# Chunked attention feeding a routed expert layer on one core: the last tiles reordered

## The chip, the cores and the metric

The kernel runs on one core of a Trainium2 chip. The metric is the device time of one execution in microseconds (us); below it is the median of several runs. The core has five engines, each with its own queue of instructions that it works off in order: PE (TensorE, matrix products; its weight loads are listed as PEld), DVE (VectorE), ACT (ScalarE), POOL (GpSimd) and SP (SyncE, which here only issues transfers). Transfers run on 16 DMA engines, and are issued by SP or by POOL.

## The reference

Four sequences of 768 positions with 8 heads of 64 go through attention in chunks of 32 queries. A chunk sees 8 memory rows and the keys from 16 before the chunk to 8 behind it. The result, 3072 tokens of 512 numbers, goes through a dense layer of two products and, beside it, through one of eight experts per token.

```python
k_full = np.concatenate([mem_k, k_ctx], axis=2)        # per chunk of 32 queries
a = softmax(scale * q_c @ k_full.T); out_c = a @ v_full
...
x = out.transpose(0, 2, 1, 3).reshape(B * S, H * D)    # 3072 x 512
y_dense = np.maximum(x @ w1_dense, 0.0) @ w2_dense
logits = x @ w_gate                                    # 8 experts
expert_idx = np.argmax(logits, axis=1); probs = softmax(logits)
y_moe[mask] = gate_w[mask, None] * (np.maximum(x[mask] @ w1[e], 0) @ w2[e])
return y_dense + y_moe
```

## The kernel before, in words

**Tiles.** The 3072 tokens are 24 tiles of 128. A loop over g = 0 to 23 (L507 to L560) does one step for each of several tiles at once: `scores` and `exp` of tile g, `turn` (transposing the softmax weights) of g-1, `values` (attention times v, normalized into `xn`, cast by POOL into a ring row) of g-2, `turn_x` and `cast_x` (transposing the token rows for the products) of g-3, and `gate` (router logits), `dense1` and `dense2` of g-4. The order in which these are written is the order in each engine's queue; nothing reorders it. What is left of the last four tiles after g = 23 is written out by hand behind the loop (L567 to L657); this is called the tail below.

**Groups.** Tiles are routed in groups, before the change seven of three, then one of two and one of a single tile (L43). When the last tile of a group has its logits, `choose` (L366) finds each token's expert as a one-hot `oh` and the weight (`es`, and its reciprocal into the ring row), all on DVE but for one exponential on ACT. `rank` (L395) counts, with products on PE, how many earlier tokens chose the same expert (`oh_sum` holds the sums over earlier groups), adds the expert's first row (`ecap`), masks by `oh` and so has each token's row in `xs`, a table in DRAM with 3200 rows per expert. `ship` (L429) lets POOL scatter one tile's rows to `xs` by an indirect transfer. Tiles below 20 (`SPLIT`) go whole, with their dense result; of tiles 20 to 23 the token part goes first and the dense part by a late scatter (L657) once `dense2` is done.

**Buffers.** The ring has six rows, so the cast of tile t waits for the scatter of tile t-6. `xn` has one buffer: the next tile's `xn` waits for the cast and for the transposes of the one before. The values' PSUM tile `xp` has one buffer too.

**Loads.** POOL issues keys and queries, and from g = 6 one half of an expert's weights per iteration (`load_w`, L545: float32 in DRAM, bfloat16 in SBUF, 16 halves). SP issues v. In iterations 18 and 20 SP also issues the front writes (L552): 128 rows ahead of each expert's tokens in `xs` are filled with finite numbers, so that a slot which begins below an expert's first token reads something harmless.

**Table and slots.** Behind the last rank, products with `ones` give the tokens per expert (L617), and about a dozen small DVE operations (L621 to L644) and a product (L646) make a table of 31 slots: first row in `xs` and expert number. Each slot is 128 rows of one expert. SP reads row numbers from the table into its registers in batches (L673: two, then six, then eight), and fetches the rows (L695). For slots 0 to 3 the token part is fetched first (L792) and the dense part after the late scatters (L794); slot 4 and later are fetched whole. A slot is turned on PE (L718), goes through its expert's two products (L741, L754), is weighted and added to the dense part by DVE (L762) and scattered to the output by POOL (L764). 27 slots are always done; four more stand behind a test that is not met here.

Of the kernel before, what the change touches and what calls it, by code (L numbers as in the profile page):

```python
# [24 lines left out]
NT = B * TPB  # L25
# [17 lines left out]
GROUPS = [3] * (NT // 3 - 1) + [2, 1]  # L43
QKB = 6
SPLIT = 20
FAR = 1.0e6
# [3 lines left out]
def kernel(  # L50
# [44 lines left out]
    ecap = const.tile([128, E], F32, name="ecap")  # L95
    oh_sum = const.tile([128, GRP, E], BF16, name="oh_sum")
# [7 lines left out]
    def constants():  # L104
# [4 lines left out]
        for e in range(E):  # L109
            nc.vector.memset(prio[:, e:e + 1], float(E - e))  # L110
            nc.vector.memset(ecap[:, e:e + 1], float(e * SPAN + 128))
        nc.gpsimd.iota(tok, [[128, NT]], base=0, channel_multiplier=1)
# [5 lines left out]
    with ExitStack() as one:  # L118
# [125 lines left out]
        def attention(g, qT, kbd):  # L244
# [98 lines left out]
            def last(part):  # L343
                if u == grp["size"] - 1:
# [4 lines left out]
                    "dense2": dense2, "choose": lambda: last(choose),  # L349
# [16 lines left out]
        def choose(grp):  # L366
# [6 lines left out]
            def st(shape, name, dt=F32):  # L373
                return small.tile(shape, dt, tag=f"{name}{k}", name=name, bufs=2 if k == GRP else 1)
# [15 lines left out]
            es = st([128, k], "es")  # L390
            nc.vector.reduce_sum(es, ex, axis=AX.X)
            nc.vector.reciprocal(grp["row"][:, :k, GW], es)
            grp["oh"] = oh

        def rank(grp):  # L395
# [5 lines left out]
            def st(shape, name, dt=F32):  # L401
                return small.tile(shape, dt, tag=f"{name}{k}", name=name, bufs=2 if k == GRP else 1)


            nc.tensor.matmul(rk, upper, oh, start=True, stop=False)
# [8 lines left out]
            nc.vector.tensor_tensor(at, rk, ecap.unsqueeze(1).to_broadcast(SH), ALU.add)  # L414
            nc.vector.tensor_tensor(at, at, oh, ALU.mult)
# [4 lines left out]
            nc.vector.tensor_tensor(oh_sum[:, :k], oh_sum[:, :k], oh, ALU.add)  # L420
# [40 lines left out]
        low = const.tile([128, E, E], F32, name="low")  # L461
        rb = const.tile([128, NSLOT + 1], F32, name="rb")

        def table_constants():
# [4 lines left out]
            nc.vector.memset(low, 0.0)  # L469
            for e in range(1, E):  # L470
                nc.vector.memset(low[:, e, :e], 1.0)
# [35 lines left out]
        for g in range(NT):  # L507
# [16 lines left out]
            do("choose", 4)  # L524
            do("dense1", 4)
# [19 lines left out]
            if g >= 6:  # L545
                load_w()
# [5 lines left out]
            if g in (18, 20):  # L552

                for e in range(g % 4 // 2, E, 2):
# [278 lines left out]
```

## Time and profile before

| | |
|---|---|
| time, median of 3 runs | 266.5 us (265.94 to 268.05) |
| the profiled execution | 267.22 us, of which 265.3 are its span |
| PE, PEld busy | 211.3, 169.1 us |
| DVE, ACT, POOL busy | 171.5, 148.2, 145.1 us |
| mean granted clock of PE | 0.929 |
| weight loads (POOL) | 16 of 512 KB, 9.5 us from issue to landing |
| scatters to `xs` | 28, median 3.6 us |
| fetches of whole slots | 23 of 385 KB, median 4.4 us |

The profile is taken on the chip in one execution. It has a page and a trace that answers questions. In the page and the answers, L12 is line 12 of the kernel before, and times are us from the start of the span. A row of the timeline has start, length, engine, line, operation, output and inputs with shape, count, and in brackets how long the engine had been idle and what ended it. A row of the chain of waits has start, length, engine and work; the chain follows the work that ended last back to what released it. Lines marked "issue" are time for which the profile names no cause. A row of stretches has the busy time of each engine in that stretch, the clock granted to PE as a share of its full speed, the mean busy share of the DMA engines and the GB/s they moved.

### The profile page before, as it was taken

How to read it: one execution, taken by the hardware profiler on the slowest of the kernel's cores; microseconds unless marked ns; L12 is line 12 of the kernel's file. 1: busy time of each engine (PE TensorE's matmuls, PEld its weight loads, DVE VectorE, ACT ScalarE, POOL GpSimd, SP SyncE). 2: the span in 40 equal slices, each digit the busy share in tenths (PEclk: the TensorE clock that was granted, in tenths of full speed). 3: DMA queues.
4: the chain of work that ended last, by engine and by line, in shares of the span. 5: the costliest groups of instructions: out<-in, count | busy, mean ns of one | idle time of the engine just before them, and what ended most of it. 6: DMA issues, size and time to landing. Idle time of an engine off the chain costs nothing.

```text
span 265.3 us, 9665 instructions
## 1 busy us (share of the span) xinstructions
PE 211.3 (80%) x3936; PEld 169.1 (64%) x3969; DVE 171.5 (65%) x415; ACT 148.2 (56%) x232; POOL 145.1 (55%) x178
## 2 busy tenths in 40 slices
PE   0554898998988799877998699689558799999960
PEld 0343686777776688665886577678446577776730
DVE  6737677778785678774686946544633576776750
ACT  3744567778777667755767467313235455655520
POOL 8997394627868335635436434316541466565660
PEclk9999999999999889997999979755988999999995
DMA  5999999868999998997999999204267899999740
GB/s 78 194 198 196 193 201 194 149 112 169 152 224 231 237 199 200 181 216 147 150 215 353 303 227 175 91 2 161 80 190 223 281 292 327 310 327 314 243 158 28
DMA packets 55948, 52.52 MB, mean 198 GB/s; under 512 B 30302, under 2 KB 48222, under 8 KB 55904
## 3 DMA queue, kind: packets, MB, share of 16 engines
q0 software_dynamic: 22768, 31.52, 56.0%
q1 hardware_dynamic: 33136, 20.38, 32.4%
q8 instruction: 32, 0.52, 0.8%
q14 instruction: 12, 0.10, 0.1%
HBM read 48.74 MB, written 19.69 MB: 258 GB/s over the span
## 4 chain that ended last, share of the span: by engine, by line
PE 42%; DMA 26%; ACT 9%; DVE 9%; issue 7%; POOL 3%; SPq 2%; POOLq 0%; DVEq 0%; ACTq 0%
DMA vw<-in_v_dram 8%; DMA xg<-xs 6%; PE pgt L323 6%; PE ph L741 6%; PE py L754 5%; DMA wall<-in_moe_w_dense_dram 5%; PE py L339 5%; PE ph L330 5%; PE xp L292 4%; DMA xs<-wall 3%; PE ap L280 3%; PE xtp L311 3%; ACT vw L200 3%; PE tp L226 3%; ACT h L333 2%
## 5 line engine op out<-in xcount | busy, mean ns | idle before, releaser
L764 POOL DMA_INDIRECT out_dram<-o,dest x27 | 31.8, 1179 | 29.1 <-DVE o L762 27.2
L304 POOL CAST ring<-xn 128x512 bf16<-128x512 f32 x24 | 16.1, 669 | 55.5 <-DVE xn L301 52.2
L447 POOL DMA_INDIRECT xs<-ring,si x28 | 29.8, 1063 | 21.6 <-DVE oh_sum L420 7.5
L318 DVE CAST xT<-xtp 128x512 bf16<-128x512 f32 x24 | 16.6, 690 | 27.8 <-ACT x L313 27.8
L762 DVE SCALAR_TENSOR_TENSOR o<-py,xg 128x512 f32<-128x512 f32 x27 | 20.3, 751 | 18.0 <-PE py L754 14.9
L292 PE MATMUL xp<-vw,aT 64*32 64x65 f32 x1536 | 24.0, 239 | 9.1 <-issue 6.9
L741 PE MATMUL ph<-xT,wa 128*128 128x128 bf16 x432 | 29.3, 222 | 1.1 <-ACT xT L720 1.1
L323 PEld LDWEIGHTS pgt<-wgate,x 128*128 128x128 f32 x192 | 27.5, 217 | 3.4 <-issue 1.8
L323 PE MATMUL pgt<-wgate,x 128*128 128x8 f32 x192 | 28.0, 273 | 1.2 <-DVE df L380 1.2
L330 PE MATMUL ph<-xT,wall 128*128 128x128 bf16 x384 | 27.2, 227 | 1.6 <-issue 1.6
L741 PEld LDWEIGHTS <-wa 128*128 128x128 bf16 x432 | 26.2, 100 | 1.6 <-issue 1.4
L330 PEld LDWEIGHTS <-wall 128*128 128x128 bf16 x384 | 25.3, 106 | 2.7 <-issue 2.4
L754 PE MATMUL py<-wall,h 128*128 (+1 forms) x97 | 26.1, 379 | 1.0 <-issue 0.5
L292 PEld LDWEIGHTS xp<-vw,aT 64*32 64x32 f32 x1536 | 18.6, 112 | 12.9 <-issue 8.4
L339 PE MATMUL py<-wall,h 128*128 128x512 bf16 x74 | 22.3, 410 | 4.3 <-ACT h L333 1.4
L720 ACT COPY xT<-xt 128x512 bf16<-128x512 bf16 x27 | 15.7, 587 | 16.2 <-PE xt L718 16.2
L237 ACT COPY kbd<-tp 64x768 bf16<-64x768 bf16 x16 | 12.7, 792 | 20.0 <-PE tp L226 18.6
L744 ACT ACTIVATE h<-ph 128x512 bf16<-128x512 f32 x27 | 16.1, 597 | 11.3 <-PE ph L741 10.9
L731 DVE COPY wa<-wall 128x2048 bf16 (+1 forms) x27 | 18.4, 685 | 5.2 <-PE ph L741 3.9
L282 ACT COPY aT<-ap 128x512 f32<-128x512 f32 x24 | 14.0, 583 | 13.4 <-PE ap L280 13.3
L275 ACT ACTIVATE a<-a 128x512 f32<-128x512 f32 x24 | 15.1, 631 | 10.0 <-DVE a L270 9.9
L200 ACT COPY vw<-vw 24x1408 f32<-24x1408 f32 x15 | 20.5, 1365 | 0.4
(119 smaller groups left out, 428.3 us busy)
## 6 DMA issues: line engine op xcount, KB each, us to landing
xg<-xs SPq DMA_DIRECT2D x23, 385.0 KB, 4.4
wall<-in_moe_w_dram POOLq DMA_DIRECT2D x16, 512.0 KB, 9.5
xs<-wall SPq DMA_DIRECT2D x8, 385.0 KB, 11.7
kb<-in_k_dram POOLq DMA_DIRECT2D x16, 192.0 KB, 7.7
qb<-in_q_dram POOLq DMA_DIRECT2D x16, 192.0 KB, 8.2
vw<-in_v_dram SPq DMA_DIRECT2D x32, 96.0 KB, 7.4
vw<-in_v_dram SPq DMA_DIRECT2D x32, 88.0 KB, 10.1
wall<-in_moe_w_dense_dram POOLq DMA_DIRECT2D x2, 512.0 KB, 12.5
```

Of the source, the lines that this page charges most:

```text
L200: copy(vw[r + 32:r + CTX, hps, :VC - 1, :D], vw[r:r + CTX - 32, hps, 1:, :D])
L292: nc.tensor.matmul(xp[32 * cc:32 * cc + 32, par, (D + 1) * hp:(D + 1) * (hp + 1)], st["aT"][r, hp, 32 * cc:32 * cc + 32], vw[r, hp, 4 * (g ...
L318: nc.vector.tensor_copy(xT, st["xtp"])
L323: nc.tensor.matmul(grp["pg"][:, u, :], st["x32"][:, d, :], wgate[:, d, :], start=(d == 0), stop=(d == DT - 1))
L330: nc.tensor.matmul(ph[:, f, :], wall[:, E, d, 128 * f:128 * f + 128], st["xT"][:, d, :], start=(d == 0), stop=(d == DT - 1))
L339: nc.tensor.matmul(py, st["h"][:, f, :], wall[:, E, DT + f, :], start=(f == 0), stop=(f == FT - 1))
L447: i = nc.gpsimd.indirect_dma_start(xs_parts[:, :] if lo else xs[:, :], bass.IndirectOffsetOnAxis(ap=grp["si3" if lo else "si"][:, t:t + 1] ...
L731: nc.vector.tensor_copy(wa, wall[:, :min(j + 1, E)][:, bass.ds(low_enough(of_dve[j], j), 1), :DT] .rearrange("p a t m -> p (a t) m"))
L741: nc.tensor.matmul(ph[:, f, :], wa[:, d, 128 * f:128 * f + 128], xT[:, d, :], start=(d == 0), stop=(d == DT - 1))
L754: nc.tensor.matmul(py, h[:, f, :], wall[:, :min(j + 1, E)][:, bass.ds(e, 1), DT + f] .rearrange("p a m -> p (a m)"), start=(f == 0), stop= ...
L762: nc.vector.scalar_tensor_tensor(o, py, xg[:, GW:GW + 1], xg[:, XW:YW], op0=ALU.mult, op1=ALU.add)
L764: i = nc.gpsimd.indirect_dma_start(out[:, :], bass.IndirectOffsetOnAxis(ap=dest[:, j:j + 1], axis=0), o, None, bounds_check=NT * 128 - 1, ...
```

## The change

- Groups are now six of three and three of two: 18 and 19, 20 and 21, 22 and 23. Tiles 18 and 19 are chosen and ranked in the loop's last iteration.
- `choose` ends with the one-hot; a new `weight` makes the normalization. In the loop it follows at once, in the tail it stands behind `rank`.
- `rank` adds the expert's first row by one more product, so DVE has one operation less. The last group doesn't add to `oh_sum`; the counts come from `oh_sum` and from the last group's one-hot (five products instead of three).
- The tail has a new order on all engines: tile 20's gate first, its dense1 early, dense1 of 21 beside the table, dense2 of 21 and cast of 23 inside the table's operations, dense1 and dense2 of 22 and 23 after them.
- The table takes fewer operations ahead of its first product (a scan for the running sum instead of a product with `low` and a reduction), and has two products instead of one: row numbers first, experts second.
- SP's batches begin with four and four instead of two and six.
- Weight loads: every second iteration from 6 to 14, each one from 15, two in 18 and in 20; the last comes in 23 instead of 21.
- The front writes stand in iterations 21 and 23 instead of 18 and 20.

```diff
-GROUPS = [3] * (NT // 3 - 1) + [2, 1]
+GROUPS = [3] * 6 + [2] * 3
...
+        def weight(grp):
+            k = grp["size"]
+            es = small.tile([128, k], F32, tag=f"es{k}", name="es")
+            nc.vector.reduce_sum(es, grp["ex"], axis=AX.X)
             nc.vector.reciprocal(grp["row"][:, :k, GW], es)
...
-            nc.tensor.matmul(rk, upper, oh, start=True, stop=False)
+            nc.tensor.matmul(rk, ones[:1], ecapb[:1].unsqueeze(1).to_broadcast([1, k, E]),
+                             start=True, stop=False)
+            nc.tensor.matmul(rk, upper, oh, start=False, stop=False)
...
-            nc.vector.tensor_tensor(at, rk, ecap.unsqueeze(1).to_broadcast(SH), ALU.add)
-            nc.vector.tensor_tensor(at, at, oh, ALU.mult)
+            nc.vector.tensor_tensor(at, rk, oh, ALU.mult)
...
-            if g >= 6:
-                load_w()
+            if (g >= 6 and g % 2 == 0) or g >= 15:
+                load_w(2 if g in (18, 20) else 1)
...
-            if g in (18, 20):
-                for e in range(g % 4 // 2, E, 2):
+            if g in (21, 23):
+                for e in range((g - 21) // 2, E, 2):
...
-        new_group(opens[NT - 1])
+        new_group(opens[NT - 2])
+        do("gate", 20)
+        ship()
         do("values", 22)
         do("turn", 23)
+        ship()
         do("turn_x", 21)
-        do("gate", 20)
         do("cast_x", 21)
+        do("dense1", 20)
         do("values", 23)
-        do("choose", 20)
         do("turn_x", 22)
+        do("cast_x", 22)
         do("gate", 21)
-        do("rank", 20)
-        ship()
-        ship()
-        ship()
+        do("choose", 21)
+        do("turn_x", 23)
         do("gate", 22)
-        do("choose", 22)
-        do("cast_x", 22)
-        do("turn_x", 23)
-        do("dense1", 20)
-        do("rank", 22)
+        do("rank", 21)
+        do("weight", 21)
         ship()
         ship()
         do("gate", 23)
         do("choose", 23)
         do("dense2", 20)
-        do("dense1", 21)
         do("rank", 23)
+        do("weight", 23)
         ship()
-        do("cast_x", 23)
-        do("dense2", 21)
+        ship()
...
-            nc.tensor.matmul(cp, ones, oh_sum[:, t, :], start=(t == 0), stop=(t == GRP - 1))
-        do("dense1", 22)
+            nc.tensor.matmul(cp, ones, oh_sum[:, t, :], start=(t == 0), stop=False)
+        for t in range(2):
+            nc.tensor.matmul(cp, ones, grps[-1]["oh"][:, t, :], start=False, stop=(t == 1))
+        do("dense1", 21)
...
-        nc.vector.tensor_tensor(m8, low, nt.unsqueeze(1).to_broadcast([128, E, E]), ALU.mult)
-        nc.vector.reduce_sum(pex, m8, axis=AX.X)
-        nc.vector.tensor_scalar(c128, cp, -128.0, None, ALU.add)
+        nc.vector.tensor_tensor_scan(pex[:, 1:], onesf[:, :E - 1], nt[:, :E - 1], 0.0,
+                                     op0=ALU.mult, op1=ALU.add)
...
+        nc.tensor.matmul(tb[:, 0], onesf, dg[:, 0], start=True, stop=True)
+        do("dense2", 21)
...
-        nc.tensor.matmul(tb, onesf, dg, start=True, stop=True)
+        nc.tensor.matmul(tb[:, 1], onesf, dg[:, 1], start=True, stop=True)
+        do("cast_x", 23)
...
+        do("dense1", 22)
         do("dense2", 22)
         do("dense1", 23)
         do("dense2", 23)
...
-    BATCHES = {0: 2, 2: 6, 8: 8, 16: 8, 24: USUAL - 24, USUAL: NSLOT - USUAL}
+    BATCHES = {0: 4, 4: 4, 8: 8, 16: 8, 24: USUAL - 24, USUAL: NSLOT - USUAL}
```

More of the change, by code (lines that the diff above doesn't have):

```diff
@@ L95 @@
     ecap = const.tile([128, E], F32, name="ecap")
+    ecapb = const.tile([128, E], BF16, name="ecapb")
     oh_sum = const.tile([128, GRP, E], BF16, name="oh_sum")
@@ L348, in attention @@
                     "turn_x": turn_x, "cast_x": cast_x, "gate": gate, "dense1": dense1,
-                    "dense2": dense2, "choose": lambda: last(choose),
+                    "dense2": dense2, "choose": lambda: last(choose), "weight": lambda: last(weight),
                     "rank": lambda: last(rank)}
@@ L373, in st @@
             def st(shape, name, dt=F32):
-                return small.tile(shape, dt, tag=f"{name}{k}", name=name, bufs=2 if k == GRP else 1)
+                return small.tile(shape, dt, tag=f"{name}{k}", name=name, bufs=3 if k < GRP and name[:2] == "si" else 2)
             lg = grp["pg"][:, :k]
@@ L524 @@
             do("choose", 4)
+            do("weight", 4)
             do("dense1", 4)
```

35 lines of the change are left out of this document (16 added, 19 removed).

## The prediction

> **What bounds the kernel now.** I read the page's top first (PE busy for 80% of the span), then busy time by stretches, then the chain of waits of the tail, then the timelines of PE, DVE, POOL and SP there. The stretches (us, busy and count of PE, PEld, DVE, ACT, POOL, then granted clock, DMA share, GB/s) show where the clock is halved:
>
> ```profile
> 155.00:160.00 5.00, 5.00 (x124) 4.33 (x124) 2.60 (x8) 3.32 (x5) 2.47 (x4) 0.89 1.03 240
> 160.00:165.00 5.00, 4.93 (x120) 4.21 (x120) 3.00 (x6) 4.13 (x6) 2.50 (x3) 1.00 0.95 130
> 170.00:175.00 5.00, 3.84 (x77) 3.25 (x76) 2.49 (x7) 0.82 (x3) 1.06 (x4) 0.50 0.22 84
> 175.00:180.00 5.00, 4.92 (x31) 4.89 (x32) 2.75 (x17) 1.05 (x4) 1.43 (x3) 0.50 0.00 0
> 215.00:220.00 5.00, 4.92 (x62) 3.71 (x62) 3.58 (x8) 2.88 (x6) 3.27 (x3) 1.00 0.94 316
> ```
>
> Three stages: a loop to 166 us, a tail of the last four tiles to 195.5 at a clock of 0.50 for most of it and with an idle DMA in its middle, and the expert slots, where PE is full again. The chain of waits (start, us, what) crosses from tail to slots so:
>
> ```profile
> 191.47 0.43 PE tb L646 x2
> 194.41 1.05 PE py L339 x4
> 196.84 2.90 DMA xs<-ring,si
> 201.98 5.37 DMA xg<-xs
> ```
>
> And PE's timeline, where that chain ends (in brackets the idle time before, and what ended it):
>
> ```profile
> 207.39 0.40 PE L718 MATMUL xt<-ident,xg 128*128 128x128 bf16 x4 [1.79 <-DMA xg<-xs]
> ```
>
> This is the chain to remember. The last dense product ends at 195.46 (call that moment X); its copy to the ring, the late scatter of tile 23, the four late fetches and then the fetch of slot 4 follow, and PE turns slot 4 at 207.39. From X to there are 11.9 us, none of which the change shortens. From 207.39 on PE is full to the end, so the end moves with X.
>
> **The change part by part.** *Front rows and expert weights.* SP's and POOL's timelines:
>
> ```profile
> 133.08 0.94 SPq L194 DMA_DIRECT2D vw<-in_v_dram  x2
> 134.11 6.94 SPq L555 DMA_DIRECT2D xs<-wall  x8
> 154.88 0.60 POOL L304 CAST ring<-xn 128x512 bf16<-128x512 f32 x1 [3.33 <-DMA xs<-ring,si]
> 163.67 1.05 POOL L447 DMA_INDIRECT xs<-ring,si  x1 [0.16 <-POOL ring L305]
> 171.02 0.61 POOL L304 CAST ring<-xn 128x512 bf16<-128x512 f32 x1 [1.01 <-DVE xn L301]
> wall<-in_moe_w_dram POOLq DMA_DIRECT2D x16, 512.0 KB, 9.5
> xs<-ring,si POOLq DMA_INDIRECT x28, 3.6
> ```
>
> The eight front writes already leave back to back, right behind the last load of v: they wait for nothing of their iteration, and SP has nothing else queued. In the changed order of SP they stand at the same place. I cost that move at zero, both ways.
>
> The weight loads do move. Iterations 7, 9, 11 and 13 lose theirs; 18 and 20 get a second one, 22 and 23 one each. What the loop may gain stands in the chain of waits, where PE waited for nothing that the profile names:
>
> ```profile
> 76.14 1.08 issue
> 82.79 0.90 issue
> 88.70 1.49 issue
> 90.00:95.00 5.00, 4.76 (x109) 4.12 (x110) 2.55 (x8) 1.33 (x3) 0.83 (x2) 0.66 1.19 233
> 117.72 3.12 issue
> q8 instruction: 32, 0.52, 0.8%
> ```
>
> I read these as PE waiting for its code, which comes by DMA (the q8 row), in stretches where the DMA share is 1.2. The first three (3.47 us) lie where every second weight load goes away, and the third is followed by a stretch at a clock of 0.66. At most all three go, and the 1.7 us that the low clock cost (0.34 of 5 us): 5.2 us. At least nothing goes, or the same waits come up later in the loop, where loads are added: +2. Keys, queries and v still load in the same stretch, so I take half of the waits alone, **-1.7 us**. The wait at 117.72, amid loads of v, stays.
>
> The price is at the other end. Between 155 and 165 POOL's queue alone moved 240 and 130 GB/s, 1.85 MB in 10 us. A weight load of 512 KB costs 2.8 us there. Two more of them stand ahead of tile 16's scatter (issued 163.67): 5.7 us. With the median of 3.6 us it now lands at 167.3, then at 173. The cast of tile 22 (0.61, at 171.02 now) overwrites that ring row, so it ends at 173.6 then, and xn of tile 23 waits for that cast, since xn has one buffer. By the sum below that xn comes at 174.6 anyway: 1.0 us of cover, so zero; if the cover is gone, every further us goes into X. In POOL's queue the last loads also stand ahead of the scatters of tiles 18 to 23: the queue is empty by 175 now, and four loads (11.3 us) later then, about 186. The cover of that is that PE is not free for slot 0 before X.
>
> *The tail.* PE's and DVE's timeline rows that carry the sum:
>
> ```profile
> 160.78 0.95 PE L323 MATMUL pgt<-wgate,x 128*128 128x8 f32 x8
> 168.14 0.85 PE L292 MATMUL xp<-vw,aT 64*32 64x65 f32 x64 [2.07 <-DVE xn L301]
> 194.41 1.04 PE L339 MATMUL py<-wall,h 128*128 128x512 bf16 x4 [0.75 <-ACT h L333]
> 178.83 0.17 DVE L378 TENSOR_REDUCE gmx<-pgt 128x2 f32<-128x16 f32 x1 [0.83 <-PE pgt L323]
> 179.95 0.17 DVE L392 RECIPROCAL ring<-es 128x2 f32<-128x2 f32 x1
> ```
>
> The chain of waits gives the times from start to start, at the halved clock and (the ph at 192.77) at the full one, and the first and last of eleven table operations:
>
> ```profile
> 171.68 1.12 PE xp L292 x64
> 177.08 1.71 PE pgt L323 x8
> 178.79 0.95 PE xtp L311 x4
> 181.56 1.71 PE pgt L323 x8
> 183.50 1.49 PE py L339 x3
> 184.99 1.71 PE ph L330 x16
> 188.58 0.18 DVE desk L621
> ...
> 190.63 0.24 DVE desk L641
> ...
> 192.77 0.91 PE ph L330 x16
> ```
>
> Choices and rank of tiles 18 and 19 move into the loop's last iteration: some 1.3 us on DVE (a choice with its weight, 178.83 to 180.12), hidden where DVE waits for ACT; an extra ACT operation delays the chain by 0.2. The gate of tile 20 (0.95) slides into the 2.07 us in which PE waits before tile 22's values, free. From 169 I assume the halved clock again, with these rates (gate and ph 1.71, py 1.49, transposes 0.95, values 1.12). PE's new order then gives: values 22 to 169.2, transposes of 23 and 21 to 170.8, dense1 of 20 to 172.5, values 23 to 173.6, transposes 22 to 174.6, gate 21 to 176.3, transposes 23 to 177.2, gate 22 to 178.9, rank, gate 23 to 180.8. DVE keeps up (its choice of 20 and 21 is ready at 176.8 for gate 22). So the last gate ends at 180.8 instead of 181.56 + 1.71 = 183.3.
>
> From there to the slot table: the choice without its weight 1.0, rank matmuls and dense2 of 20 ahead of them 0.6, at, sl, si and the weight's two operations 1.1, and nine table operations instead of eleven (188.58 to 190.87, 0.21 each; the scan has no row, one of 0.16 to 0.4 as the neighbours, I take 0.21) 1.9: 4.7 us, where now 183.3 to 191.47 are 8.2. Counts no longer wait for oh_sum, and tile 23 is no longer ranked alone behind dense2 and dense1. The table's matmul comes at 185.5: 6.0 us earlier.
>
> But more dense work stands behind it. Now 4.0 us follow (191.47 to X: one py, one ph, a wait for ACT of 0.75, one py). Then follow py of 21 (1.05), the second table matmul, and twice ph 0.9, ACT 0.75, py 1.05, which nothing fills: 6.9 us at full clock. X = 192.5: **-2.9 us**. Bounds: -6.5 if the tail runs at full clock (worked out below), +3 if the ring wait binds 6 us past its cover.
>
> *Start of the slots.* SP now reads four table entries before its first fetch and the next four ahead of slot 4's fetch, not after slot 1's:
>
> ```profile
> 193.61 3.36 SPq L705 DMA_DIRECT2D xg<-xs  x4
> 199.87 1.92 SPq L699 DMA_DIRECT2D xg<-xs  x4
> xg<-xs SPq DMA_DIRECT2D x23, 385.0 KB, 4.4
> ```
>
> Four fetches with such a read among them took 3.36 us, four without 1.92: the read is 1.4 us. Where it is now it hides, since SP then waits for the late scatters anyway; there it stands on the chain. But slot 4's fetch takes 5.37 us where the median is 4.4, since it queues behind the late fetches' data: about 1.0 of the 1.4 passes while it would queue. From 0 to 1.4, I take **+0.5**. That the tables come 6 us earlier buys nothing here: slots 0 to 3 start sooner and then wait for slot 4.
>
> *The rest:* the added rank matmul is tiny on PE, each rank loses one DVE operation of 0.2, constants change a few operations before 20 us where DMA is the limit: zero.
>
> Sum: -1.7 - 2.9 + 0.5 = -4.1 us against the profiled execution's 267.22 (span 265.3): 263.1. That execution stands 0.7 above the median of the runs, 266.5; how much of that is chance one execution can't tell, so I keep the sum and forecast **263.0 us** against 266.5. A change of 1% (2.7 us) is about what a measurement of this kernel can tell from none.
>
> **The rivals.** *Nothing gained in the loop.* The waits for code might not come from the weight loads: the longest, at 117.72, stands amid loads of v. Then 267.22 - 2.9 + 0.5 = 264.8. The Trainium skill, "DMA: Bandwidth & Descriptors", section on queues, rings and completion order, speaks for this rival: an engine takes its queues in turn by packets, so a deep POOL queue would hold another queue's packet up little. No row here separates the two.
>
> *Clock lost again at the slots.* PE waits 1.79 us before slot 4 without losing its clock. With the first slots unhindered it may wait 2.3 to 3.2; one window at 0.50 costs what it cost at 90 us, 1.7: 264.7.
>
> *Slower: the ring.* The place is the cast of tile 22. For: the one such wait, 3.33 us at 154.88, came after one load per iteration, with front writes beside. Against: the front writes are long done by then. The time is 263.1 plus what tile 16's scatter lands after 174.0 (173 and the cover): from 178.1 on nothing is gained, and at 181 it is 270.1.
>
> *Full clock in the tail.* Dense1 of 20 between transposes and values may lift the clock at 173. Then gates take 0.95 and transposes half of theirs, xn of tile 23 waits for the ring until 173.7, choice and gates follow, the last gate ends at 177.5, the table comes at 182.0 and X at 188.9, -6.5: 267.22 - 1.7 - 6.5 + 0.5 = 259.5. The Trainium skill, "TensorE: Matmul & The Clock Gate", Part 1, gives the half clock only after an idle window of some 3.4 us, by which this rival would be sure; the trace is against it as a rule, for here 2.07 us of idle PE stood before 15 us at 0.50.
>
> **How the numbers follow.** Chances: forecast 0.40, nothing gained in the loop 0.20, clock lost 0.10, ring 0.18, full clock 0.12. Faster by over 1% (under 263.8) is most of the first and all of the last: 0.47. Slower by over 1% (above 269.2) is most of the ring, 0.14. Within 1%: 0.39. Likeliest case alone: 261.5 to 264.5. The range takes in full clock at its lower end and half of the ring's cases: 259.5 to 268.5.
>
> **What would show it.** Right: front writes still back to back behind the last v load; the table's first matmul 5 to 7 us earlier against the loop's end; X some 3 us earlier; slot 4's turn 12 us behind X; weight loads until about 180. The loop step: fewer unnamed waits between 70 and 95. Wrong: a cast on POOL waiting for a scatter after 170 by more than 4 us, an xn behind it, or a clock of 0.50 after slot 4's turn.

## The result and the profile after

The first comparison gave 263.85 us as the median of 12 executions of the changed kernel (256.09 to 269.35) against 267.78 for the kernel before (264.94 to 275.09). Its ratio, 0.960 (95% interval 0.953 to 0.967), leaves out executions well above each kernel's fastest; that kept two of the twelve, 256.1 and 256.8, so all executions are given here as well. Over the study the same two kernels ran 28 and 65 times: medians 262.9 and 267.7, ratio 0.982 (0.978 to 0.991, by resampling the executions of all chips as one pool).

The forecast of 263.0 us is next to the median, but the execution that was profiled first, 256.75 us (span 255.0), is 10.5 us below the 267.22 of the kernel before, where the sum had 4.1. The trace of that execution, by stretches (us, busy and count of PE, PEld, DVE, ACT, POOL, granted clock, DMA share, GB/s):

```profile
155.00:160.00 5.00, 4.13 (x104) 3.62 (x104) 2.79 (x10) 2.63 (x5) 1.58 (x4) 1.00 1.17 270
160.00:165.00 5.00, 3.25 (x81) 2.83 (x81) 2.35 (x7) 0.89 (x3) 4.05 (x6) 0.87 1.13 209
170.00:175.00 5.00, 4.02 (x33) 2.72 (x32) 2.90 (x19) 1.18 (x2) 3.05 (x4) 0.50 0.25 88
175.00:180.00 5.00, 4.25 (x36) 3.22 (x35) 3.17 (x12) 1.57 (x3) 2.53 (x5) 0.76 0.63 195
```

From 163.7 to 177.4 the tail is again at the halved clock. The chain of waits of the tail (start, us, what):

```profile
150.10 8.29 DMA xs<-ring,si
163.98 1.11 PE xtp L313 x4
178.54 1.04 PE py L341 x4
```

A scatter that takes 8.29 us to land (median before 3.6) now stands at its head. The timelines of PE, POOL and DVE:

```profile
153.93 1.03 PE L341 MATMUL py<-wall,h 128*128 128x512 bf16 x4
158.51 0.61 POOL L306 CAST ring<-xn 128x512 bf16<-128x512 f32 x1 [3.26 <-DMA xs<-ring,si]
160.46 0.76 POOL L86 DMA_DIRECT2D wall<-in_moe_w_dram  x1
161.52 1.04 POOL L454 DMA_INDIRECT xs<-ring,si  x1 [0.30 <-issue]
162.55 0.65 POOL L306 CAST ring<-xn 128x512 bf16<-128x512 f32 x1
163.23 0.69 DVE L303 TENSOR_TENSOR xn<-xp,rs 128x512 f32<-128x512 f32 x1 [2.14 <-POOL ring L306]
163.98 1.11 PE L313 MATMUL xtp<-identf,xn 128*128 128x128 f32 x4 [1.75 <-DVE xn L303]
173.77 0.60 PE L647 MATMUL tb<-desk,onesf 128*128 128x31 f32 x2 [0.98 <-DVE desk L650]
181.22 1.04 PE L341 MATMUL py<-wall,h 128*128 128x512 bf16 x4 [0.75 <-ACT h L335]
193.96 0.40 PE L726 MATMUL xt<-ident,xg 128*128 128x128 bf16 x4 [4.36 <-DMA xg<-xs]
194.19 1.67 PE L749 MATMUL ph<-xT,wa 128*128 128x128 bf16 x16
```

The cast of tile 21 waits for that scatter's ring row until 158.51. A scatter, a weight load and another scatter follow in POOL's queue, so tile 22's cast comes at 162.55, the last `xn` behind it at 163.23, and PE idles 1.75 us for it; from there the gates take 1.85 us instead of about 1.0. SP's timeline:

```profile
125.15 1.85 SPq L196 DMA_DIRECT2D vw<-in_v_dram  x2
127.09 7.51 SPq L564 DMA_DIRECT2D xs<-wall  x8
176.76 1.95 SPq L713 DMA_DIRECT2D xg<-xs  x4
186.57 3.05 SPq L707 DMA_DIRECT2D xg<-xs  x4
190.16 2.75 SPq L713 DMA_DIRECT2D xg<-xs  x4
```

The loop's last dense product (`py` of tile 19) ends at 154.96, before at 166.07: 11.1 us earlier. X stands at 182.26, that is 27.3 behind the loop's end instead of 29.4. Slot 4 turns 11.7 behind X (11.9 before). X to the end of the span takes 72.8 instead of 69.9. So -11.1 - 2.1 + 2.9 = -10.3 in the span: the loop's gain, since the other two nearly cancel.

Two things make up those 11.1 us. From the first dense product to the loop's end, before and after:

```profile
43.60:166.10 122.50, 108.44 (x2526) 89.59 (x2544) 87.37 (x195) 84.53 (x133) 65.72 (x84) 0.96 1.03 202
42.00:155.00 113.00, 106.63 (x2553) 87.53 (x2552) 87.82 (x197) 84.48 (x134) 64.62 (x83) 1.00 1.00 202
```

One is the clock. The loop of the kernel before has three stretches of 3.4 us at 0.50, from 91.2, 121.9 and 152.7, behind unnamed waits of 1.49, 3.12 and 1.98 us; at half speed 10.2 us do the work of 5.1. The execution after has none from 36 to 163.6. The other is the waits themselves: those of PE for which the profile names no cause, of half a us or more and between 59 and 160, sum to 8.6 us before and 2.0 after.

### The profile page after: what moved, and what is told of

Same layout as the page of the kernel before. It is cut to its first block, busy times and chain, and to the rows that moved or that the text cites. A ratio compares the mean times of both kernels' runs of the same rounds, so it can differ in the third digit from the quotient of the medians.

```text
span 255.0 us, 9707 instructions
## 1 busy us (share of the span) xinstructions
PE 208.3 (82%) x3982; PEld 163.8 (64%) x3982; DVE 170.5 (67%) x399; ACT 147.9 (58%) x232; POOL 144.0 (56%) x178
## 4 chain that ended last, share of the span: by engine, by line
PE 34%; issue 19%; POOL 16%; ACT 12%; DVE 9%; DMA 7%; POOLq 1%; ACTq 0%; DVEq 0%
POOL out_dram L772 12%; PE py L341 6%; PE pgt L325 6%; PE ph L332 5%; PE xp L294 5%; PE ap L282 3%; DMA qb<-in_q_dram 3%; DMA xs<-ring,si 3%; ACT vw L202 3%; PE xtp L313 3%; PE tp L228 3%; ACT h L335 2%; DVE xT L320 2%; PE sc L261 2%; ACT x L315 2%
## 5 line engine op out<-in xcount | busy, mean ns | idle before, releaser
L306 POOL CAST ring<-xn 128x512 bf16<-128x512 f32 x24 | 15.4, 643 | 48.3 <-DVE xn L303 36.8
L770 DVE SCALAR_TENSOR_TENSOR o<-py,xg 128x512 f32<-128x512 f32 x27 | 20.3, 750 | 23.4 <-PE py L762 18.2
L762 PE MATMUL py<-wall,h 128*128 (+1 forms) x108 | 28.6, 388 | 0.0
L341 PE MATMUL py<-wall,h 128*128 128x512 bf16 x96 | 26.4, 400 | 1.5 <-ACT h L335 1.5
L325 PEld LDWEIGHTS pgt<-wgate,x 128*128 128x128 f32 x192 | 25.4, 203 | 1.9 <-issue 0.2
L325 PE MATMUL pgt<-wgate,x 128*128 128x8 f32 x192 | 26.0, 262 | 0.0
L294 PEld LDWEIGHTS xp<-vw,aT 64*32 64x32 f32 x1536 | 18.0, 107 | 9.0 <-issue 5.7
L752 ACT ACTIVATE h<-ph 128x512 bf16<-128x512 f32 x27 | 16.1, 597 | 11.1 <-PE ph L749 11.1
L303 DVE TENSOR_TENSOR xn<-xp,rs 128x512 f32<-128x512 f32 x24 | 16.6, 692 | 7.9 <-POOL ring L306 5.9
L284 ACT COPY aT<-ap 128x512 f32<-128x512 f32 x24 | 14.0, 584 | 12.6 <-PE ap L282 12.5
## 6 DMA issues: line engine op xcount, KB each, us to landing
xs<-wall SPq DMA_DIRECT2D x8, 385.0 KB, 10.2
```

What stands on the lines that cost most here:

```text
L294: nc.tensor.matmul(xp[32 * cc:32 * cc + 32, par, (D + 1) * hp:(D + 1) * (hp + 1)], st["aT"][r, hp, 32 * cc:32 * cc + 32], vw[r, hp, 4 * (g ...
L325: nc.tensor.matmul(grp["pg"][:, u, :], st["x32"][:, d, :], wgate[:, d, :], start=(d == 0), stop=(d == DT - 1))
L341: nc.tensor.matmul(py, st["h"][:, f, :], wall[:, E, DT + f, :], start=(f == 0), stop=(f == FT - 1))
L762: nc.tensor.matmul(py, h[:, f, :], wall[:, :min(j + 1, E)][:, bass.ds(e, 1), DT + f] .rearrange("p a m -> p (a m)"), start=(f == 0), stop= ...
L770: nc.vector.scalar_tensor_tensor(o, py, xg[:, GW:GW + 1], xg[:, XW:YW], op0=ALU.mult, op1=ALU.add)
```

## The experiments

The unmodified kernels were profiled several times too. Three moments from PE's timeline carry the rest of this document: the end of the loop's last dense product, X, and the end of the span.

| kernel | loop end | loop end to X | X to end | span |
|---|---|---|---|---|
| before | 166.1 | 29.4 | 69.9 | 265.3 |
| before, again | 170.2 | 27.3 | 70.5 | 268.0 |
| before, third | 164.8 | 26.4 | 72.4 | 263.6 |
| changed | 155.0 | 27.3 | 72.8 | 255.0 |
| changed, again | 166.2 | 21.7 | 72.0 | 259.9 |
| changed, third | 165.1 | 26.3 | 71.6 | 263.0 |
| changed, fourth | 166.1 | 28.0 | 71.6 | 265.7 |
| new pacing alone | 166.5 | 29.5 | 69.1 | 265.1 |
| changed, old pacing | 172.8 | 28.3 | 71.9 | 273.0 |
| no loads up to 14 | 161.4 | 40.0 | 71.2 | 272.6 |
| two loads, 6 to 13 | 168.0 | 23.8 | 71.9 | 263.7 |
| changed, no loads | 157.6 | 27.6 | | 291.3 |
| before, no loads | 158.4 | 26.4 | | 291.3 |
| six early slots | 163.7 | 23.4 | 70.1 | 257.2 |
| six early, again | 165.8 | 24.8 | 69.8 | 260.4 |
| old table read | 169.6 | 27.8 | 72.2 | 269.6 |
| two loads last | 169.3 | 24.6 | 74.8 | 268.7 |
| load of 16 at 9 | 163.4 | 27.7 | 67.2 | 258.3 |
| loads in the gap | 163.7 | 23.1 | 71.0 | 257.8 |
| both | 162.6 | 26.2 | 68.4 | 257.2 |

Seven of these runs have the changed kernel's loop to the letter: the four of that kernel, the old table read and the two with six early slots. Their loops end between 155.0 and 169.6, in the mean at 164.5; the three of the kernel before end between 164.8 and 170.2, in the mean at 167.0.

**The pacing alone, and all but the pacing.** The kernel before with this edit, and the changed kernel with its reverse:

```diff
-            if g >= 6:
-                load_w()
+            if (g >= 6 and g % 2 == 0) or g >= 15:
+                load_w(2 if g in (18, 20) else 1)
```

> The kernel before with the new pacing of the weight loads and nothing else. Theory A (the 11 us that the loop lost come from the pacing: with every second weight load gone, PE's code arrives in time): the last PE row of tile 19's dense product ends near 155 instead of 166.1, the unnamed waits at 76 to 90, 117.7 and 150.5 are gone, and with the old tail behind it the time is 255 to 260. Theory B (the loop gained from the split of choice and weight or from the choices of tiles 18 and 19 inside the loop, not from the pacing): loop end at 164 to 166, time 265 to 268. What the prediction had: -1.7, so 265.5.

Measured: median 266.7 (262.6 to 270.2) beside 267.8 for the kernel before, ratio 0.993 (0.985 to 1.002); loop end 166.5.

> The changed kernel with one weight load in each iteration from 6 on, as before. Theory A: the unnamed PE waits come back, loop end at 164 to 166, and what is left is the tail's 2.1 us and the slots: 264 to 267. Theory B: loop end stays near 155 to 157, time 256 to 259. The ring wait in the tail (cast on POOL behind a scatter at 158.5, 3.26 us) should shrink in both, since no load is doubled.

Measured: median 268.3 (266.2 to 274.7), ratio 1.009 (1.004 to 1.015); loop end 172.8. Neither half shows a gain by itself, and a loop end of 155, which Theory A had expected, did not come back with the pacing. PE's unnamed waits of over half a us between 59 and 106 us are one with the new pacing (1.0), two with the old (0.5 and 1.4, and 1.2 at 109), which fits Theory A; those at 117 to 152 are in both (4.2 and 4.7 us).

**The table read.** `BATCHES = {0: 4, 4: 4, ...}` back to `{0: 2, 2: 6, ...}`:

> The changed kernel with the slot table read 2 and 6 again instead of 4 and 4. By the prediction the read on the chain costs 0.5 (0 to 1.4), so this is 0.5 faster than the changed kernel, within 256 to 257. If the read is hidden behind the late scatters' data, no difference; if the first reads matter, slot 4's turn moves by up to 1.4 us against the end of the last dense product.

Measured: median 267.9 (260.9 to 271.3), not the 256 to 257 expected; the profiled loop ended at 169.6, which this edit doesn't touch. SP's timeline of this run, where the late scatter of tile 23 is issued at 198.80:

```profile
190.18 3.48 SPq L713 DMA_DIRECT2D xg<-xs  x4
201.71 1.92 SPq L707 DMA_DIRECT2D xg<-xs  x4
203.81 3.96 SPq L713 DMA_DIRECT2D xg<-xs  x4
```

The read moves as forecast: the first four fetches take 3.48 here and 1.95 in the changed kernel, the late ones reach from issue to issue 2.1 us here and 3.6 there. So the new batches put slot 4's fetch 1.5 us later behind the late fetches, as forecast (1.4). PE turns slot 4 at 209.95, 12.5 behind X, where the four profiles of the changed kernel have 11.7, 12.3, 12.0 and 11.8: the later fetch shows no cost. That the read's time passes while the fetch would have queued fits this, and is argued.

**Two loads behind the last late scatter** instead of the doubled ones in 18 and 20:

```diff
-                load_w(2 if g in (18, 20) else 1)
+                load_w()
...
         late = [scatter(grp, t, XW, YW) for grp, t in rest]
+        load_w(2)
```

> The changed kernel without the second load in iterations 18 and 20; these two loads are issued behind the last late scatter. If the doubled loads cause the ring wait (the casts on POOL that wait 7.08 and 3.26 us for a scatter at 149 and 158), the cast at 158.5 comes 2 to 5 us earlier, xn of tile 23 with it, and X by 2 us: 254 to 255 fast. If the ring wait has another cause (the front writes, the scatters themselves), no difference in the tail; then the two loads among the slots' fetches can cost 1 to 2 us at slots 0 to 7.

Measured: median 270.4 (265.5 to 271.9), ratio 1.003 (0.995 to 1.011). X came 24.6 behind the loop's end and no cast waits for a scatter after 160, but the loads stand ahead of slot 4's fetch in the DMA engines, and PE waited 8.28 us for it (X to end 74.8). POOL's and SP's timelines:

```profile
196.24 1.67 POOL L86 DMA_DIRECT2D wall<-in_moe_w_dram  x2
201.10 7.59 SPq L714 DMA_DIRECT2D xg<-xs  x4
```

**The changed kernel again**, beside fresh runs of the kernel before:

> The changed kernel itself, word for word, once more. Its runs so far spread from 256.1 to 269.4 with a median of 263.9, those of the kernel before from 263.8 to 275.4 with a median of 267.8. Theory C (both kernels lose a chance number of PE waits for code in the loop, each with a stretch at the halved clock behind it; what the change itself gives is the 4 us between the medians, and the 10 us of the first comparison came from an execution without such waits): median 262 to 266, spread again over 8 us or more. Theory A (the new pacing removes the waits for good): all runs at 256 to 259.

Measured: median 261.1 (258.8 to 265.3) against 270.3 (261.8 to 275.4) on that chip, ratio 0.990 (0.984 to 0.997). Theory A, every execution at 256 to 259, falls. Theory C fits better, though the median is 0.9 us under its 262 and the spread 6.5 us instead of 8. The profile shows another kind of execution. PE's and POOL's timelines:

```profile
119.30 0.46 PE L294 MATMUL xp<-vw,aT 64*32 64x65 f32 x11 [3.11 <-issue]
165.22 1.03 PE L341 MATMUL py<-wall,h 128*128 128x512 bf16 x4
171.13 0.64 POOL L306 CAST ring<-xn 128x512 bf16<-128x512 f32 x1
173.27 0.61 POOL L306 CAST ring<-xn 128x512 bf16<-128x512 f32 x1 [0.17 <-DMA xs<-ring,si]
174.07 1.03 PE L325 MATMUL pgt<-wgate,x 128*128 128x8 f32 x8 [0.32 <-DVE df L382]
176.17 1.52 PE L341 MATMUL py<-wall,h 128*128 128x512 bf16 x4
186.91 1.04 PE L341 MATMUL py<-wall,h 128*128 128x512 bf16 x4 [0.75 <-ACT h L335]
200.26 0.48 PE L726 MATMUL xt<-ident,xg 128*128 128x128 bf16 x4 [4.99 <-DMA xg<-xs]
```

The wait at 117 is back, the loop is as long as before (166.2), and the tail is not: the last two casts wait 0.2 us at most, the gates take 1.04, X stands 21.7 behind the loop's end. Two executions of one kernel: one with a loop 11 us shorter and a slow tail, one the reverse.

**What the weight loads do to the loop.** No loads in iterations 6 to 14 and two in each from 15 on; then two in each from 6 to 13:

```diff
-            if (g >= 6 and g % 2 == 0) or g >= 15:
-                load_w(2 if g in (18, 20) else 1)
+            if g >= 15:
+                load_w(2)
```

> The changed kernel with no weight load in iterations 6 to 14 and two in each from 15 on. If weight loads are what makes PE's code late (theory A), the loop up to tile 10 has no unnamed PE wait and its dense product ends by 102 in every profile, with the waits back after 15 (loop end 157 to 160) and a longer ring wait. If the code comes late without them as well (theory C), waits of 1 to 3 us stand between 40 and 122 as in the earlier runs. Time 258 to 266 in either case, since the late loads cost 0 to 5 us at the ring.

> The changed kernel with two weight loads in each iteration from 6 to 13 and none after. Theory A: waits for code between 62 and 110, several of 1 to 3 us, dense product of tile 10 at 112 or later, none after 115; the ring wait of the tail (7.08 and 3.26 us on POOL at 149 and 158) goes, since only the scatters are in POOL's queue then, and X comes 2 us earlier against the loop's end. Theory C: no more waits in the loop than elsewhere; time 260 to 266.

Measured: medians 269.0 (265.8 to 274.4; ratio 1.017, 1.011 to 1.024) and 268.9 (263.4 to 271.9; 1.007, 0.999 to 1.015). Stretches of 10 us of the late loads:

```profile
70.00:80.00 10.00, 10.00 (x272) 8.61 (x272) 7.76 (x21) 7.82 (x14) 6.79 (x10) 1.00 0.95 177
100.00:110.00 10.00, 9.72 (x261) 8.61 (x260) 7.79 (x19) 7.61 (x14) 6.33 (x7) 1.00 0.35 105
140.00:150.00 10.00, 8.01 (x181) 6.45 (x181) 7.19 (x21) 4.74 (x10) 4.15 (x7) 1.00 1.19 227
```

And of the early loads:

```profile
70.00:80.00 10.00, 8.91 (x192) 7.34 (x190) 7.79 (x19) 7.27 (x13) 8.01 (x12) 1.00 1.21 216
100.00:110.00 10.00, 8.84 (x243) 7.74 (x242) 6.51 (x14) 7.58 (x11) 4.08 (x8) 1.00 1.20 220
140.00:150.00 10.00, 10.00 (x232) 8.31 (x221) 7.86 (x17) 7.04 (x10) 3.15 (x5) 1.00 0.86 273
```

Of the stretches of 10 us from 60 on (to 160 with the late loads, to 170 with the early ones), those with a DMA share of 1.1 or more have PE busy for 7.6 to 9.3 us, those under 1.0 for 9.1 to 10.0, and they change places with the loads. PE's unnamed waits of over half a us follow: with the late loads none from 63 to 133 and five from 133 to 160, with the early ones eight from 72 to 134 (the longest 2.38) and none from there to 169. So the waits come where the weight loads are, as Theory A has it. A high DMA share alone does not bring them: in the first execution of the changed kernel two such stretches have PE nearly full.

```profile
70.00:80.00 10.00, 9.86 (x199) 7.81 (x194) 8.73 (x18) 8.66 (x14) 5.80 (x10) 1.00 1.20 219
120.00:130.00 10.00, 9.98 (x256) 8.38 (x255) 7.93 (x23) 7.20 (x13) 4.56 (x8) 1.00 1.21 206
```

The Trainium skill, "DMA: Bandwidth & Descriptors", section on queues, rings and completion order, spoke for the rival that nothing is gained in the loop, since an engine takes its queues in turn by packets; the stretches of these two runs do not bear out that conclusion, since PE waits where POOL's queue is deep. The dense product of tile 10, expected by 102 and at 112 or later, ended at 106.0 and 114.6. The late loads missed their time (258 to 266) by the ring: a cast waits 10.20 us for a scatter, PE 3.41 and 2.89 us for an `xn`, and X stands 40.0 behind the loop's end. With the early loads no cast waits for the ring, and it stands 23.8 behind.

**Neither loads nor their pace.** All sixteen expert loads behind the last late scatter, in both kernels:

```diff
-            if (g >= 6 and g % 2 == 0) or g >= 15:
-                load_w(2 if g in (18, 20) else 1)
...
         late = [scatter(grp, t, XW, YW) for grp, t in rest]
+        load_w(16)
```

> The changed kernel with all sixteen expert loads taken out of the loop and issued behind the last late scatter: its loop and tail run without them, and its slots then wait for them, so the time itself (285 to 310) says nothing and only the moments are read. If full DMA engines are what makes PE wait for its code, no unnamed wait over 1 us stands between 50 and 170, the DMA share stays under 1.0 there, and the last dense product of the loop ends at 152 to 158, as in the first execution of the changed kernel (155.0). If the waits near 117 come without weight loads too, the loop ends at 160 or later. Tail: with no load ahead of a scatter no cast waits for the ring, and X stands 20 to 23 us behind the loop's end.

> The kernel before with the same: all sixteen expert loads behind its last late scatter. If its loop differs from that of the changed kernel by the weight loads alone, it ends at 152 to 158 here too, within 2 us of the other. Its tail then shows what the new order is worth by itself: if the old tail falls to the halved clock by its own order, X stands 28 to 30 us behind the loop's end, as in the kernel before (29.4) and in the one with the new pacing alone (29.5), against 20 to 23; if the ring or the loads had made it slow, 21 to 25.

Measured: the loops end at 157.6 and 158.4, within 1 us. Neither has an unnamed wait of half a us between 59 and 160 or a stretch at half speed between 43 and 160. Two stretches of the changed kernel:

```profile
100.00:110.00 10.00, 9.55 (x250) 7.82 (x249) 7.60 (x19) 7.26 (x13) 5.79 (x7) 1.00 0.47 142
110.00:120.00 10.00, 9.75 (x219) 8.17 (x226) 7.51 (x14) 8.76 (x14) 4.29 (x7) 1.00 0.23 72
```

No wait near 117 stands in either, nor with the late loads. In the 16 profiles with about one weight load per iteration at that time (all of this study but those two and the pair of late and early loads), it is 1.5 to 3.4 us in 14, 0.74 in one and absent in one: the first execution of the changed kernel. So, as far as one profile of each can tell, the loops of the two kernels differ only by the loads. The tail was the surprise: X stands 27.6 behind the loop's end with the new order and 26.4 with the old. PE's timeline of the changed kernel:

```profile
156.78 0.81 PE L341 MATMUL py<-wall,h 128*128 128x512 bf16 x3
163.73 0.85 PE L294 MATMUL xp<-vw,aT 64*32 64x65 f32 x64 [2.21 <-DVE xn L303]
168.00 1.85 PE L325 MATMUL pgt<-wgate,x 128*128 128x8 f32 x8
176.82 0.61 PE L645 MATMUL tb<-desk,onesf 128*128 128x31 f32 x2 [0.98 <-DVE desk L643]
184.15 1.04 PE L341 MATMUL py<-wall,h 128*128 128x512 bf16 x4 [0.75 <-ACT h L335]
```

Of the kernel before:

```profile
157.61 0.81 PE L339 MATMUL py<-wall,h 128*128 128x512 bf16 x3
180.79 0.43 PE L644 MATMUL tb<-desk,onesf 128*128 128x62 f32 x2 [2.34 <-DVE desk L642]
183.73 1.04 PE L339 MATMUL py<-wall,h 128*128 128x512 bf16 x4 [0.75 <-ACT h L333]
```

After a wait of 2.2 us for `xn`, with no load near and the ring free, the new tail goes at half speed too. DVE's row of that `xn` has it wait for `ph`, the dense1 of tile 20 that the new order puts there:

```profile
162.89 0.69 DVE L303 TENSOR_TENSOR xn<-xp,rs 128x512 f32<-128x512 f32 x1 [1.00 <-PE ph L332]
```

(The second execution has the same order and no such wait.) The table comes 19.2 instead of 22.4 us behind the loop's end, and 8.4 us pass from there to X instead of 4.0: the gain is given back. The two are not equals, though: the new tail ran 13.7 us at half speed, the old one 6.8, by estimate a difference of 3.4 us in X. That the loads alone make the tail slow falls with the new tail.

**Six slots fetched early.** An attempt at the 4.4 to 5.0 us that PE waits for slot 4:

```diff
-    BATCHES = {0: 4, 4: 4, 8: 8, ...
+    BATCHES = {0: 8, 8: 8, ...
-            xg = w3.tile([128, YW], F32, tag="xg", name="xg")
+            xg = w3.tile([128, YW], F32, tag="xg", name="xg", bufs=8)
-                if j + 4 < hi:
-                    fetch(j + 4)
+                if j + 6 < hi:
+                    fetch(j + 6)
-        for j in range(4):
+        for j in range(6):
```

> The changed kernel with the first six slots fetched ahead of the late scatters instead of four (eight fetch buffers, the table read in one batch of eight). If PE's 4.36 us at slot 4 wait for a fetch that is queued behind the late scatters and late fetches, as the chain says, PE goes on to slots 4 and 5, the wait falls to 0 to 2 us, the halved clock behind it goes too (1.6), and the time falls by 3 to 6 us against the changed kernel. If the late words themselves set the pace (o of slot 0 waits for them, and the buffers with it), the wait only moves to slot 6: 0 to 2 us gained.

> The kernel with six early slots once more, as the measure for the three others on this chip: 252 to 259 with a median near 257.8 if the chips agree.

Measured: medians 257.8 (252.5 to 258.9) and, on another chip, 259.7 (254.0 to 262.3). Over the twelve executions 258.6, against 262.9 for the 28 of the changed kernel: ratio 0.984 (0.971 to 0.989). X to end falls from 72.0 (mean of four) to 69.9. SP's and PE's timelines:

```profile
183.15 3.11 SPq L713 DMA_DIRECT2D xg<-xs  x6
191.38 2.97 SPq L707 DMA_DIRECT2D xg<-xs  x6
202.31 0.40 PE L726 MATMUL xt<-ident,xg 128*128 128x128 bf16 x4 [2.69 <-DMA xg<-xs]
```

The wait has moved to slot 6 and is 2.7 and 2.5 us in the two profiles. It is the fastest version found.

**Loads in other places**, all with six early slots. The load of 16 moved to 9; the two doubled loads behind the scatters of 20 and 21, where the DMA engines have room; and both:

```diff
-            if (g >= 6 and g % 2 == 0) or g >= 15:
-                load_w(2 if g in (18, 20) else 1)
+            if g != 16 and (g in (6, 8, 9, 10, 12, 14) or g >= 15):
+                load_w(2 if g in (18, 20) else 1)
```

> The kernel with six early slots, with the weight load of iteration 16 moved to iteration 9. PE's wait near 113 to 120 (1.97, 2.60, 2.67, 3.11, 3.42 us in five profiles, absent in the kernel without loads up to 14) falls where loads of v and weight loads run together. If the weight loads are what makes the code late there, this wait goes or falls under 1 us, with the halved clock behind it: loop end 3 to 5 us earlier, median 254 to 256 against 257.8. If loads of v alone do it, or the load at 9 makes another wait, no difference.

> The kernel with six early slots, without the second loads at 18 and 20; these two are issued behind the scatters of tiles 20 and 21, where the DMA engines stand mostly idle (share 0.27 at 175 to 180). If the doubled loads cause the ring wait, no cast on POOL waits more than 1 us for a scatter after 160, the last xn comes without waiting, the tail keeps the full clock, and X stands 21 to 23 us behind the loop's end even where the loop is fast: median 255 to 257. If the ring wait has another cause, the tail stays at 23 to 27 and the median at 257 to 259.

> Both edits together (no load at 16, one at 9; the doubled loads moved behind the scatters of 20 and 21). If the two waits are independent, the gains add: median 252 to 255, lowest below 251. If a faster loop runs into the ring wait, as in the first execution of the changed kernel, the gain of the loop is given back in the tail and the median stays at 256 to 258.

Measured: 260.6 (260.1 to 266.0), 260.3 (253.7 to 266.0) and 259.7 (258.2 to 261.4), beside 259.7 with neither: no difference that these runs can tell, and none of the medians expected if the moves helped (254 to 256, 255 to 257, 252 to 255). Loop ends 163.4, 163.7 and 162.6. The wait at 117 was 2.63, 2.38 and 0.74, so one load fewer does not remove it reliably. Without the doubled loads the last two casts wait 0.3 us at most, and X stands 23.1 and 26.2 behind the loop's end: no ring wait, and still two speeds of the tail (3.4 and 13.7 us at 0.50). With the doubled loads moved alone, PE then waits 4.82 us for the rows of slot 0.

**How far single executions lie apart.** The unmodified kernels once more, for the table:

> The kernel before, word for word, for a second profile. Read are two moments: the end of the loop's last dense product (166.1 in the first profile) and from there to X (29.4). If the loop's term is a shift of the whole distribution by the pacing, this loop ends at 164 to 172, later than those of the changed kernel on average; if it is chance alone, anywhere from 155 to 172 in both kernels. The tail: 28 to 30 if the old order holds it at the halved clock, 22 to 30 if that is chance as well.

> The same again, with the same expectations: loop end at 164 to 172 and 28 to 30 from there to X, or, by chance alone, 155 to 172 and 22 to 30.

> The changed kernel, word for word, for a third profile (loop end 155.0 and 166.2 so far, from there to X 27.3 and 21.7). If loop and tail trade against each other (a fast loop runs into a slow tail), a loop end of 160 goes with 24 to 26; if they are independent, any pair of 155 to 168 and 21 to 28.

> The same again, with the same expectations: the pair of loop end and distance to X lies on the line from (155.0, 27.3) to (166.2, 21.7), or anywhere between 155 to 168 and 21 to 28.

Measured: on this chip the medians were 265.6 for the kernel before (13 executions) and 263.9 for the changed one (10), 1.7 apart, where they lay 3.9 and 9.3 apart in the two comparisons above; the ratio, from eight of the ten, is 0.997 (0.991 to 1.004). Loop ends and tails are in the table. They do not lie on one line (166.2 goes with 21.7, 166.1 with 28.0), so loop and tail do not simply trade. The old tails of 27.3 and 26.4 us lie under the 28 to 30 expected if the old order held them at half speed.

## Why the prediction was wrong, point by point

*The loop, -1.7 us: the step that failed.* In the first execution the loop gained 11.1 us, and the two executions that the ratio of 0.960 keeps are that one and one of 256.1. The step took the waits of one profile for a fixed property of the program. It bounded the gain at 5.2 us, three waits and one stretch at half speed, and said "The wait at 117.72, amid loads of v, stays". In that execution this wait went as well, and that of 2.0 us at 150.5, and with them all three stretches at half speed, worth 5.1 us, of which the sum had counted one. The longest wait stayed in the three other profiles (3.1, 3.3, 2.9 us), and so did one near 40 (1.8 to 2.0) that the first lacks.

In the mean the term was less far off: four loop ends (163.1) against three (167.0) make -3.9, all seven with that loop (164.5) -2.5, while single executions of that loop lie 14.7 apart. So no mean here tells -1.7 from these. PE's unnamed waits of half a us or more between 59 and 106 sum to 3.5, 2.8 and 2.2 in the three profiles before, and there is none in the four after. Up to 160 they sum to 8.6, 11.5 and 5.0 before and to 2.0, 4.6, 3.8 and 4.2 after, 4.7 less in the mean. They do not set the loop's end alone: the run with the old table read has one of 2.6 in that stretch and ends at 169.6, with 17.1 us at half speed between 42 and 131. That the waits come with the loads is shown; that what is late is PE's code, as I read it, is argued only, since the rows name no cause.

*The forecast beside the median.* That 263.0 lies next to 263.85 is partly luck. The mean terms of the four profiles (-3.9, -1.9 and +1.0 from X to the end) add up to -4.8, near the forecast's -4.1, but the single spans lie from 10.3 below to 0.4 above the 265.3 of the first profile before.

*The tail, -2.9 us.* -2.1 in the first execution, -1.9 in the mean (25.8 against 27.7), but the term hides two cases: 21.7 with most of the tail at the full clock, 26.3 to 28.0 otherwise. Between the loop's end and X the clock stood at 0.50 for 17.1, 13.7 and 6.8 us before and for 13.7, 3.4, 13.7 and 12.1 after. The fast one is the rival "full clock in the tail" (bound -6.5, here -6.0 against the mean before), to which I gave 0.12; but dense1 of 20 lifted nothing, the clock stayed full from the loop until 176.6. The table's place was right: it came 18.8, 14.9, 17.8 and 16.9 us behind the loop's end, in the three profiles before 25.4, 23.3 and 21.8, so 6.4 earlier in the mean. As forecast, the dense work behind it gives most of that back: from the table to X the sum had 6.9 us at full speed, and it took 8.5, 6.8, 8.5 and 11.1. Without weight loads it gives back all of the gain. So the new order alone is not shown to gain.

*The ring, priced at nothing.* In the first execution the wait came one tile earlier than I had put it, at the cast of tile 21, and passed on through POOL's queue to the cast of 22 and the last `xn`: PE lost 1.75 us. It came where the loop was 11 us faster and the loads were not; I had reckoned the cover against a loop that ends near 166. With such loops the last cast waits 0.17 us (166.2) or not at all (166.1); with 165.1 the casts of 21 and 23 wait 3.30 and 1.03, and PE waits for neither. The step also took the median landing of all 28 scatters, 3.6 us, for scatters beside weight loads: those issued from 128.7 to 153.4 in the first execution took 8.3 to 14.5, and the kernel before already had 10.0 and 8.5 at 144.8 and 149.7.

*The slots, +0.5.* Slot 4 turns 11.9, 11.7 and 11.4 behind X before and 11.7, 12.3, 12.0 and 11.8 after: +0.3. But X to the end grew by 1.0 in the mean (70.9 to 72.0). In the four profiles PE waits 4.36, 4.99, 4.19 and 3.32 us for slot 4, before 1.79, 0.78 and 2.74, since slots 0 to 3 are done sooner. Each time it then runs 3.4 us at half speed (in the first `ph` 1.67, `py` after it 1.91): the rival of the lost clock, which came beside the forecast instead of in its place. But the kernel before loses as much behind X in its three profiles (197.0 to 200.4 in the first), so this does not explain the 1.0 us.

*The front rows, zero.* Right: SP's rows show them behind the last load of v, back to back.

*The clock.* Half speed followed 1.75 us of idle PE in the first execution and 2.2 without loads. In the other three profiles of the changed kernel it came at 176.6, 173.0 and 175.2 with no wait of PE over 0.45 us since the loop's end; in the 3.4 us ahead PE was busy for 3.08, 2.73 and 3.03. So the ring's wait is not what slows these tails. The Trainium skill, "TensorE: Matmul & The Clock Gate", Part 1, asks for an idle window of some 3.4 us; these rows do not bear that out. What does come back in every profile here is 3.4 us: it, or a multiple of it, is the length of each stretch at half speed. What makes the tail fall to half speed in some executions stays open, as does why the waits near 40 and 117 are missing in one execution.

## What to carry to other kernels

Read a second and a third profile of the same program before you trust a term: here the loop of one program ended 11 us apart in two executions, more than the medians of the two kernels ever did. A load that nothing waits for can still cost the engine that bounds the loop: without weight loads PE's unnamed waits were gone from it, and with two per iteration they stood where the loads were. But moving the loads moved the waits, and spreading them alone is not shown to pay (ratio 0.993, up to 1.002). Take a transfer's time from the stage in which it will run: 3.6 us was the median of all scatters, and those of the loop's last iterations took 8.3 to 14.5. What is gained upstream is measured again at the next fixed moment, here a ring row that comes free when the loads ahead of it have landed.

## What was not expected of the hardware

- With two weight loads per iteration PE was busy for 7.6 to 9.3 of 10 us where they ran (DMA share 1.1 or more), and for 9.1 to 10.0 in the same loop where the share was under 1.0; yet in another execution it was busy for 9.98 at 1.21.
- PE fell to half speed after being busy for 3.08 of the 3.4 us ahead, and stayed there for 3.4 us or a multiple of it, up to 17.1 in the tails of the two kernels.
- One program spread over 256.1 to 269.4 us, and in three comparisons the medians of the two kernels lay 3.9, 9.3 and 1.7 us apart (the last: 263.9 in 10 executions against 265.6 in 13).
